# A recurrent attention followed by an MLP mixer: engine order taken from the order of the kernel's pieces

## The chip, the cores and the metric

The kernel runs on one core of a Trainium2 chip. Such a core has a matrix engine (PE, which also loads weights, shown as PEld), a vector engine (DVE), a scalar engine (ACT), a general engine (POOL) and a queue that only issues transfers here (SP). Each takes its own list of instructions; semaphores tie the lists together. The metric is the device time of one execution in microseconds (us).

## The reference

The first half is a linear attention with a decay for each channel (RWKV-6), for 4 batches, 8 heads, 768 tokens and 48 channels. The second half is an MLP mixer over tokens and then over channels. All in float32; the four weight matrices come as 64-bit floats.

```python
for t in range(S):
    cur = np.einsum('bhd,bhe->bhde', u[None] * kt, vt)
    y[:, :, t] = np.einsum('bhd,bhde->bhe', rt, state + cur)
    state = wt[:, :, :, None] * state + np.einsum('bhd,bhe->bhde', kt, vt)
...
xt = x.transpose(0, 2, 1)
h = np.maximum(xt @ w_tok1, 0.0) @ w_tok2
u = x + h.transpose(0, 2, 1)
h2 = np.maximum(u @ w_ch1, 0.0) @ w_ch2
return u + h2
```

## The kernel before, in words

**Attention units.** The 4 x 768 tokens are cut into 12 units of 256 tokens, three to a batch (NU is 12). A unit has two chunks c of 128 tokens, each of two halves of 64. Heads lie in pairs, so that most matmuls of the attention use quarter tiles of PE (64 x 64).

`levels(i)` builds, for unit i, the weights between tokens of one half: six levels, in each of which blocks of 1, 2, 4 ... 32 tokens are joined. `begin` makes on ACT the copies `rp` and `kp` (L195, L199) for level 0. `gram0` and `gram` (L211, L225) multiply k and r on PE into the PSUM tiles `gram` (pool ps_g, two buffers); `join` (L250 to L252) multiplies k and r in place by decays on DVE, so it has to come after the gram of its level and before the gram of the next; `pick` moves the products into `at`, on DVE for levels 0 to 3 (L217, L234) and on ACT for levels 4 and 5 (L242).

`post(i)` uses them. For each chunk, `tokens` transposes k on PE (L284) and copies it on ACT (L286, `kT`); `carry` multiplies it with v (L296, `kv_ps`) and then updates the state on DVE, a multiplication and an addition for each half (L303 to L306). Then `before` (L318) adds what earlier states give to `y_ps`, ACT copies one column (L324, `seen`), `within` (L331) adds the unit's own weights, and ACT writes the result to `x` (L334). `kv_ps` and `y_ps` share one PSUM buffer (ps_a, tag "a"). The last two pieces of post(i) issue the loads of unit i+3 on SP: six transfers of r, k and w and one of v, into the buffers that unit i used.

**Mixing.** For each batch: `hidden` (L353), `back` (L360, with an addition on DVE, L362), `turn` (a transpose, L367, copied by ACT, L368), `up` (L375, evicted by ACT, L377) and `down` (L384, added by DVE, L388, and stored from SP, L389). `up` and `down` go by three segments of 256 tokens.

**Weights.** `convert` brings one piece of a 64-bit matrix in by a transfer on SP into `d64` (two buffers) and makes it float32 with one operation of ACT (L155) and six of DVE (L156 to L161). There are 28 pieces: 3 of w_tok1, 4 of w_tok2, 9 of w_ch1 and 12 of w_ch2. All are converted during batch 0.

**Order.** Work is written as lists of pieces, each a cost and a function. `woven` merges lists so that each is spread evenly by its costs; `emit` calls the functions. Units 0 and 1 come first, then unit 2's levels woven with the posts of units 0 and 1, the hidden pieces of batch 0 and the conversion of w_tok1, then the rest of batch 0 woven with the other conversions. After that the mixing of each batch is woven with the attention of the next: three units with batch 0's last 52 us of matmuls, three with all of batch 1's and of batch 2's. Batch 3's mixing stands alone. In the kernel before, calling a piece only records its instructions. The framework's scheduler then chooses, for each engine, which of the instructions that are ready by its own planning goes next. So the order on an engine isn't that of the pieces: grams of one level lie cut in several runs between other matmuls, and joins of units 3 to 5 lie between the conversions.

```python
    p0, p1, p2 = post(0), post(1), post(2)
    p1[4:4] = hiddens[0] + hiddens[1]
    p2[4:4] = hiddens[2] + hiddens[3]
    emit(woven(levels(2), p0 + p1, to_tok1))
    emit(woven(p2[:-4], to_tok2[:2]))
    emit(p2[-4:-2] + hiddens[4] + p2[-2:] + hiddens[5])
```

Of the kernel before, what the change touches and what calls it, by code (L numbers as in the profile page):

```python
# [10 lines left out]
f32 = mybir.dt.float32  # L11
# [8 lines left out]
C = S // 128  # L20
UC = 2
# [13 lines left out]
def woven(*lists):  # L35

    keyed = []
    for n, pieces in enumerate(lists):
        total, at = sum(c for c, _ in pieces), 0.0
        for i, (c, f) in enumerate(pieces):  # L40
            keyed.append(((at + c / 2) / total, n, i, c, f))
            at += c
    return [(c, f) for *_, c, f in sorted(keyed, key=lambda e: e[:3])]


def emit(pieces):
    for _, f in pieces:
        f()


@with_exitstack
def rwkv6_then_mixer(
    ctx: ExitStack,
# [20 lines left out]

    nc = tc.nc
    pe, dve, act, pool, sp = nc.tensor, nc.vector, nc.scalar, nc.gpsimd, nc.sync

    const = ctx.enter_context(tc.tile_pool(name="const", bufs=1))
    wts = ctx.enter_context(tc.tile_pool(name="wts", bufs=1))
# [6 lines left out]
    ps_a = ctx.enter_context(tc.tile_pool(name="ps_a", bufs=1, space=bass.MemoryType.PSUM))  # L86
# [9 lines left out]
    def load_rkw(i):  # L96
        if i >= NU:
            return
        for n, t in enumerate((rs[i % 3], ks[i % 3], ws[i % 3])):
            for rows in (slice(0, 128),) if i < 3 else (slice(0, D), slice(P, P + D)):  # L100
                sp.dma_start(t[rows], rkw[i, n, rows, :])

    def load_v(i, queue=sp):
        if i >= NU:
            return
        vs[i] = vpool.tile([128, UC, DM], f32, name="vt")
        b, j = divmod(i, UB)
        queue.dma_start(vs[i], v[b, ts(j, UC * 128), :].rearrange("(c p) e -> p c e", p=128))

    u_col = const.tile([128, A], f32, name="u_col")  # L110
    act.dma_start(u_col, u)
    load_rkw(0)
    load_rkw(1)

# [56 lines left out]
    live = {}  # L171
# [98 lines left out]
    def post(i):  # L270
        bt, half = divmod(i, UB)
        at = weights_at[i % 3]
        r_, k_ = rs[i % 3], ks[i % 3]

        def tokens(c):
            if half == 0 and c == 0:
                xs[bt] = xpool.tile([128, C, DM], f32, name="x")
            L = live[i]
            if bt == 0:
                ps = ps_g.tile([128, 2, 512], f32, name="gram")[:, 0, :].rearrange("p (a t) -> p a t", a=A)  # L280
            else:
                ps = ps_m.tile([128, A, 128], f32, name="kT_ps", tag="m")
            for a in range(A):
                pe.transpose(ps[:, a, :], k_[:, ts(c * A + a, 128)], ident)  # L284
            L["kT"] = apool.tile([128, A, 128], f32, name="kT")
            act.copy(L["kT"], ps)  # L286

        def carry(c):
            L, vt = live[i], vs[i]
            ch = half * UC + c  # L290
            last = ch == C - 1
            kv = ps_a.tile([128, 2, 512], f32, name="kv_ps", tag="a")
            for a in range(A):
                for j, q in ((0, 0), (1, 1), (0, 1), (1, 0)):
                    if not (last and j == 1):
                        pe.matmul(kv[ts(q, P), j, ts(a, D)], L["kT"][ts(j, T), a, ts(q, P)],  # L296
                                  vt[ts(j, T), c, ts(2 * a + q, D)], start=True, stop=True)
            for j in range(1 if last else 2):
                g = 2 * ch + j
                new = apool.tile([128, A, D], f32, name="state", bufs=5)  # L300
                got = kv[:, j, :A * D].rearrange("p (a e) -> p a e", a=A)
                if g == 0:
                    dve.tensor_copy(new, got)  # L303
                else:
                    dve.tensor_mul(new, state[bt, g], L["w"][:, c, :, j].unsqueeze(2).to_broadcast([128, A, D]))
                    dve.tensor_add(new, new, got)  # L306
                state[bt, g + 1] = new

        pairs = ((0, 0), (1, 1), (1, 0), (0, 1))

        def before(c):

            ch = half * UC + c
            y = live[i]["y"] = ps_a.tile([128, 2, 512], f32, name="y_ps", tag="a")
            got = [(q, j) for q, j in pairs if 2 * ch + j > 0]
            for a in range(A):
                for q, j in got:
                    pe.matmul(y[ts(j, T), q, ts(a, D)], r_[q * P:q * P + D, ds((c * A + a) * 128 + j * T, T)],  # L318
                              state[bt, 2 * ch + j][q * P:q * P + D, a, :], start=(a == 0), stop=False,
                              skip_group_check=True)  # L320
            seen = apool.tile([128, 2], f32, name="seen")
            for j in range(2):
                if (0, j) in got:
                    act.copy(seen[ts(j, T)], y[ts(j, T), :, A * D - 1])  # L324

        def within(c):
            ch = half * UC + c
            vt, y = vs[i], live[i].pop("y")
            for a in reversed(range(A)):
                for q, j in pairs:  # L330
                    pe.matmul(y[ts(j, T), q, ts(a, D)], at[ts(j, T), q, c * A + a, :],  # L331
                              vt[ts(j, T), c, ts(2 * a + q, D)], start=(2 * ch + j == 0 and a == A - 1), stop=a == 0,
                              skip_group_check=True)
            act.copy(xs[bt][:, ch, :].rearrange("p (a q e) -> p q a e", a=A, q=2),  # L334
                     y[:, :, :A * D].rearrange("p q (a e) -> p q a e", a=A))

        pieces = []
        for c in range(UC):
            pieces += [(0.5, lambda c=c: tokens(c)), (0.5, lambda c=c: carry(c))]
        for c in range(UC):  # L340
            pieces += [(0.5, lambda c=c: before(c)), (1.0, lambda c=c: within(c))]
        return pieces + [(0.01, lambda: load_rkw(i + 3)), (0.01, lambda: load_v(i + 3))]
# [61 lines left out]
    hiddens, turned, ups, downs = mixing(0)  # L404
    hiddens = [list(e) for e in zip(*hiddens)]
    to_tok1, to_tok2 = conversion(wtok1, w_tok1, 2, 256), conversion(wtok2, w_tok2, 1, 384)
    to_ch1, to_ch2 = conversion(wch1, w_ch1, 1, 512), conversion(wch2, w_ch2, 1, 384)
    emit(woven(levels(0), levels(1)))
    load_v(0)
    load_rkw(2)  # L410
    load_v(1)
    load_v(2)
    p0, p1, p2 = post(0), post(1), post(2)
    p1[4:4] = hiddens[0] + hiddens[1]
    p2[4:4] = hiddens[2] + hiddens[3]
    emit(woven(levels(2), p0 + p1, to_tok1))
    emit(woven(p2[:-4], to_tok2[:2]))
    emit(p2[-4:-2] + hiddens[4] + p2[-2:] + hiddens[5])


    for bt in range(B):
        if bt == 0:
            emit(woven(turned, to_tok2[2:] + to_ch1[:3]))
            both = [f for e in zip(ups[0], ups[1]) for f in e]
            emit(woven(both, to_ch1[3:] + to_ch2[:6]))
            emit(woven(downs[0][:-4], to_ch2[6:]))
            pieces = downs[0][-4:] + ups[2] + downs[1] + downs[2]
        else:
            hiddens, pieces, ups, downs = mixing(bt)
            pieces = [(3.9, lambda h=h: emit(h)) for h in hiddens] + pieces + ups[0]  # L430
            for s in range(1, S // SEG):
                pieces += ups[s] + downs[s - 1]
            pieces += downs[-1]
        n = (bt + 1) * UB
        if n < NU:
            att = levels(n)
            for i in range(n, n + UB - 1):
                att += woven(levels(i + 1), post(i))
            att += post(n + UB - 1)
            emit(woven(att, pieces))  # L440
        else:
            emit(pieces)
# [29 lines left out]
```

## Time and profile before

| what | us |
|---|---|
| median of 3 runs (lowest, highest) | 694.05 (691.95, 696.34) |
| the profiled execution, its own time | 687.6 |
| its span in the trace | 685.6 |
| PE busy in the span | 641.6 (94%) |
| DVE busy | 293.1 (43%) |
| ACT busy | 194.8 (28%) |

The page's slices show how this is spread. Each digit is the busy share of one fortieth of the span (17 us) in tenths; PEclk is the clock that PE was granted.

```profile
PE   3889998996799999999999999999999999999998
DVE  5998899998821435442242305442132211000000
PEclk9997898998899999999999999999999999999999
```

PE is the fullest engine over the whole span, and DVE over the first eleven slices. The costliest groups are the matmuls of the channel mixing. A group's columns are line, engine, operation, output and inputs, shape and count, then busy time, the mean of one, and the idle time of the engine before it.

```profile
L375 PE MATMUL z_ps<-xT,wch 128*128 128x256 f32 x864 | 203.2, 389 | 3.5 <-DVE wch L161 3.0
L384 PE MATMUL h_ps<-wch,z 128*128 128x384 f32 x576 | 198.6, 498 | 3.7 <-DVE wch L161 3.5
L225 PE MATMUL gram<-r,k 48*64 48x32 f32 x3840 | 85.2, 235 | 13.1 <-DVE r L251 8.5
```

Matmuls overlap, so the mean duration of one is more than what it adds to the span; how many pass in a given time is read from the chain of waits or the order of time.

### The profile page before, as it was taken

To read this page: it belongs to the slowest core of one execution; us is meant where nothing else is said; L and a number is where in the kernel's file an instruction comes from. 1 tells how busy PE (TensorE), PEld (TensorE's weight loads), DVE (VectorE), ACT (ScalarE), POOL (GpSimd) and SP (SyncE) were. 2 spreads that over 40 slices of the span, in tenths; PEclk is the share of its full clock that TensorE was granted. 3 is DMA by queue.
4 is the path that set the end of the run, shared out by engine and by line. 5 is a ranking of instruction groups with operands and counts; after the bars stand their busy time and mean duration, and the time that the engine had idled before them with its cause. 6 is when DMAs were issued, how large, how long until landed. Compare 5 with 4: busy or idle time off the path is not lost.

```text
span 685.6 us, 18835 instructions
## 1 busy us (share of the span) xinstructions
PE 641.6 (94%) x8584; PEld 466.9 (68%) x8584; DVE 293.1 (43%) x585; ACT 194.8 (28%) x489; POOL 7.2 (1%) x32
## 2 busy tenths in 40 slices
PE   3889998996799999999999999999999999999998
PEld 3877656863586666788677656788677655786854
DVE  5998899998821435442242305442132211000000
ACT  7144533441242123432321303432211201220200
POOL 3000000000000000000000000000000000000000
PEclk9997898998899999999999999999999999999999
DMA  9244544332202131110210312000000000000000
GB/s 345 69 107 132 146 140 126 124 115 71 70 25 81 36 95 48 25 25 5 80 35 3 94 35 60 2 2 2 13 13 2 25 12 12 1 0 12 12 16 31
DMA packets 16111, 38.56 MB, mean 56 GB/s; under 512 B 2176, under 2 KB 8320, under 8 KB 16032
## 3 DMA queue, kind: packets, MB, share of 16 engines
q1 hardware_dynamic: 15888, 37.36, 17.9%
q8 instruction: 67, 1.10, 0.7%
q14 instruction: 12, 0.10, 0.0%
q10 hardware_dynamic: 144, 0.00, 0.0%
HBM read 32.64 MB, written 4.72 MB: 54 GB/s over the span
## 4 chain that ended last, share of the span: by engine, by line
PE 87%; DVE 9%; issue 2%; ACT 1%; DMA 1%; SPq 0%; DVEq 0%; ACTq 0%
PE z_ps L375 29%; PE h_ps L384 28%; PE gram L225 9%; PE h_ps L353 5%; PE h_ps L360 5%; PE y_ps L331 4%; PE kv_ps L296 2%; PE y_ps L318 2%; DVE r L251 1%; DVE k L250 1%; PE kT_ps L284 1%; PE gram L211 1%; PE xT_ps L367 1%; DVE at L217 1%; DMA w<-in_rkw_dram 1%
## 5 line engine op out<-in xcount | busy, mean ns | idle before, releaser
L375 PE MATMUL z_ps<-xT,wch 128*128 128x256 f32 x864 | 203.2, 389 | 3.5 <-DVE wch L161 3.0
L384 PE MATMUL h_ps<-wch,z 128*128 128x384 f32 x576 | 198.6, 498 | 3.7 <-DVE wch L161 3.5
L375 PEld LDWEIGHTS z_ps<-xT,wch 128*128 128x128 f32 x864 | 161.4, 192 | 28.4 <-DVE wch L161 3.2
L384 PEld LDWEIGHTS h_ps<-wch,z 128*128 128x128 f32 x576 | 107.9, 192 | 73.1 <-DVE wch L161 3.7
L377 ACT ACTIVATE z<-z_ps 128x256 f32<-128x256 f32 x144 | 55.1, 383 | 177.3 <-PE z_ps L375 177.2
L225 PEld LDWEIGHTS gram<-r,k 48*64 48x64 f32 x3840 | 76.5, 152 | 34.7 <-issue 24.3
L225 PE MATMUL gram<-r,k 48*64 48x32 f32 x3840 | 85.2, 235 | 13.1 <-DVE r L251 8.5
L388 DVE TENSOR_TENSOR o<-x,h_ps 128x384 f32<-128x384 f32 x24 | 13.3, 554 | 181.9 <-PE h_ps L384 181.9
L250 DVE TENSOR_TENSOR k<-k,decay 112x512 f32<-112x512 f32 x36 | 24.9, 691 | 62.2 <-PE gram L225 62.2
L242 ACT COPY at<-gram 16x256 f32<-16x256 f32 (+1 forms) x72 | 31.2, 434 | 44.7 <-PE gram L225 37.3
L250 DVE TENSOR_TENSOR k<-k,w 112x512 f32<-112x512 f32 x36 | 24.8, 688 | 39.6 <-PE gram L225 32.9
L360 PE MATMUL h_ps<-h,wtok 128*128 128x384 f32 x96 | 36.0, 503 | 1.8 <-DVE x L362 1.8
L353 PE MATMUL h_ps<-x,wtok 128*128 128x384 f32 x96 | 37.0, 520 | 0.0
L331 PEld LDWEIGHTS y_ps<-vt,at 64*64 64x64 f32 x768 | 26.2, 142 | 9.9 <-ACT seen L324 6.3
L234 DVE COPY_PREDICATED at<-mask,gram 128x512 f32<-128x512 uint8 x36 | 32.3, 897 | 0.0
L251 DVE TENSOR_TENSOR r<-r,w 112x512 f32<-112x512 f32 x36 | 24.7, 686 | 16.5 <-ACT rp L195 16.5
L331 PE MATMUL y_ps<-vt,at 64*64 64x48 f32 x768 | 29.2, 227 | 2.1 <-ACT seen L324 1.8
L211 PE MATMUL gram<-rp,kp 48*64 48x64 f32 x768 | 20.1, 246 | 11.1 <-ACT kp L199 8.0
L211 PEld LDWEIGHTS gram<-rp,kp 48*64 48x64 f32 x768 | 17.1, 154 | 16.4 <-ACT kp L199 10.4
L217 DVE COPY_PREDICATED at<-mask,gram 128x512 f32<-128x512 uint8 x24 | 16.7, 725 | 25.7 <-PE gram L211 25.4
L155 ACT ACTIVATE size<-d 128x384 f32<-128x384 f32 (+1 forms) x28 | 17.0, 608 | 28.2 <-DMA d<-in_w_ch_dram 13.3
L324 ACT COPY seen<-y_ps 64x2 f32<-64x2 f32 x44 | 6.8, 154 | 63.6 <-PE y_ps L318 63.3
(50 smaller groups left out, 429.1 us busy)
## 6 DMA issues: line engine op xcount, KB each, us to landing
vt<-in_v_dram SPq DMA_DIRECT2D x12, 384.0 KB, 3.9
d<-in_w_ch_dram SPq DMA_DIRECT2D x9, 512.0 KB, 3.6
d<-in_w_ch_dram SPq DMA_DIRECT2D x12, 384.0 KB, 3.0
out_dram<-o SPq DMA_DIRECT2D x24, 192.0 KB, 1.9
w<-in_rkw_dram SPq DMA_DIRECT2D x18, 192.0 KB, 3.5
k<-in_rkw_dram SPq DMA_DIRECT2D x18, 192.0 KB, 3.5
r<-in_rkw_dram SPq DMA_DIRECT2D x18, 192.0 KB, 3.4
r<-in_rkw_dram SPq DMA_DIRECT2D x3, 512.0 KB, 6.1
```

The costliest lines, as they stand in the source:

```text
L211: pe.matmul(g[cols, q, ts(a, T)], L["kp"][rows, tokens], L["rp"][rows, tokens], start=True, stop=True)
L225: fours(lambda q, j, rows, cols: pe.matmul(g[cols, q, ts(ca, 32)], k_[rows, ds(ca * 128 + j * T, T)], right[rows, ts(2 * ca + j, 32 // b), ...
L234: dve.copy_predicated(out=dst, data=g.rearrange("p q (m b) -> p q m b", b=b), mask=masks[l].rearrange("p x t -> p (x t)").rearrange("p (m ...
L242: act.copy(at[p:p + b, :, :, n * 2 * b + b:(n + 1) * 2 * b], g[p:p + b, :, :, ts(n, b)])
L250: dve.tensor_mul(left, left, wv[:, :, 1].unsqueeze(2).to_broadcast([ROWS, n, b]))
L251: dve.tensor_mul(right, right, wv[:, :, 0].unsqueeze(2).to_broadcast([ROWS, n, b]))
L331: pe.matmul(y[ts(j, T), q, ts(a, D)], at[ts(j, T), q, c * A + a, :], vt[ts(j, T), c, ts(2 * a + q, D)], start=(2 * ch + j == 0 and a == A ...
L353: pe.matmul(sums[i], wtok1[:, c, ts(i, 128)], xs[bt][:, c, :], start=(c == 0), stop=(c == C - 1))
L360: pe.matmul(ps, wtok2[:, i, ts(c, 128)], h1[:, i, :], start=(i == 0), stop=(i == DTOK // 128 - 1))
L375: pe.matmul(ps, wch1[:, m, ts(jt, 128)], xT[:, m, ts(s, SEG)], start=(m == 0), stop=(m == DM // 128 - 1))
L377: act.activation(zs[s][:, jt, :], ps, AF.Relu)
L384: pe.matmul(ps, zs[s][:, jt, ts(n, 128)], wch2[:, jt, :], start=(jt == 0), stop=(jt == NJ - 1))
```

## The change

`emit` moves into the kernel's function. After each piece, it looks at the instructions that the piece has recorded and ties each to the one before it on the same engine, with a dependency that needs no semaphore. So the scheduler can no longer choose: every engine's list, SP's and POOL's among them, is in the order of the pieces. What was recorded before the first piece (masks, first loads) is tied in the same way at the first call. The state update leaves `carry` and becomes a piece of its own, which `post` places one piece later. The insertion of the hidden pieces moves by two places for this. Last, one small ACT operation on a new tile `touched` stands ahead of the first loads, so that ACT's function table is loaded then.

```diff
-def emit(pieces):
-    for _, f in pieces:
-        f()
...
+    block = nc.cur_bb.bb
+    last, done = {}, len(block.instructions)
+    behind = mybir.DependencyInfo(mybir.DependencyClass.NoSync, mybir.DependencyReason.DATA)
+
+    def emit(pieces):
+
+        nonlocal done
+        for _, f in pieces:
+            f()
+            traced = block.instructions
+            for ins in traced[done:]:
+                if ins.engine in last:
+                    tc.add_manual_dep(ins, last[ins.engine], behind, reason="order of the pieces")
+                last[ins.engine] = ins.name
+            done = len(traced)
...
     act.dma_start(u_col, u)
+    touched = const.tile([1, 2], f32, name="touched")
+    dve.memset(touched, 0.0)
+    act.mul(touched[:, 1:], touched[:, :1], touched[:, :1])
     load_rkw(0)
     load_rkw(1)
...
-            kv = ps_a.tile([128, 2, 512], f32, name="kv_ps", tag="a")
+            kv = L["kv"] = ps_a.tile([128, 2, 512], f32, name="kv_ps", tag="a")
             for a in range(A):
                 for j, q in ((0, 0), (1, 1), (0, 1), (1, 0)):
                     if not (last and j == 1):
                         pe.matmul(kv[ts(q, P), j, ts(a, D)], L["kT"][ts(j, T), a, ts(q, P)],
                                   vt[ts(j, T), c, ts(2 * a + q, D)], start=True, stop=True)
-            for j in range(1 if last else 2):
+
+        def update(c):
+            L = live[i]
+            ch = half * UC + c
+            kv = L.pop("kv")
+            for j in range(1 if ch == C - 1 else 2):
                 g = 2 * ch + j
...
-        pieces = []
-        for c in range(UC):
-            pieces += [(0.5, lambda c=c: tokens(c)), (0.5, lambda c=c: carry(c))]
+        pieces = [(0.5, lambda: tokens(0)), (0.5, lambda: carry(0)), (0.5, lambda: tokens(1)), (0.1, lambda: update(0)),
+                  (0.5, lambda: carry(1)), (0.1, lambda: update(1))]
         for c in range(UC):
             pieces += [(0.5, lambda c=c: before(c)), (1.0, lambda c=c: within(c))]
...
-    p1[4:4] = hiddens[0] + hiddens[1]
-    p2[4:4] = hiddens[2] + hiddens[3]
+    p1[6:6] = hiddens[0] + hiddens[1]
+    p2[6:6] = hiddens[2] + hiddens[3]
```

## The prediction

> **What bounds the kernel now.** I read the span cut at its own milestones first, then the chain of waits, then the order of time on DVE and on SP. The stretches below end where the last weight is converted (183.9 us) and where the first matmul of each batch's token mixing stands in the chain (254.84, 411.90 and 568.80 us). Columns: the stretch, its length, busy time (instructions) of PE, weight load, DVE, ACT, POOL, then granted clock, DMA share, GB/s.
>
> ```profile
> 0.00:38.00 38.00, 24.42 (x772) 22.86 (x772) 28.97 (x57) 18.30 (x45) 6.32 (x24) 1.00 0.58 206
> 38.00:92.00 54.00, 48.42 (x1135) 37.11 (x1135) 47.39 (x103) 25.64 (x65) 0.33 (x3) 0.87 0.47 134
> 92.00:184.00 92.00, 76.37 (x967) 55.62 (x965) 84.76 (x169) 29.06 (x65) 0.00 (x0) 0.91 0.34 101
> 184.00:255.00 71.00, 69.65 (x931) 49.34 (x932) 22.94 (x49) 19.17 (x51) 0.33 (x3) 1.00 0.22 60
> 255.00:412.00 157.00, 155.99 (x2211) 111.97 (x2211) 53.06 (x102) 45.24 (x118) 0.22 (x2) 1.00 0.14 39
> 412.00:569.00 157.00, 155.42 (x2151) 111.49 (x2152) 49.29 (x96) 39.43 (x103) 0.00 (x0) 1.00 0.05 16
> ```
>
> From 255 us on, PE is busy 155 to 156 of 157 us: there is nothing for an order to fill. Before 184 us DVE is the fuller engine (84.76 of 92) and PE stands idle 35 us in all (38-24.4, 54-48.4, 92-76.4). So the change is decided in the first 184 us, by DVE. The order of time on DVE shows how a conversion costs two prices: alone, and mixed with other work.
>
> ```profile
> 111.51 0.69 DVE L161 SCALAR_TENSOR_TENSOR wch<-size,scale 128x512 f32<-128x512 f32 x1
> 112.12 0.42 DVE L156 TENSOR_SCALAR cut<-d 128x512 uint32<-128x512 uint32 x1
> ...
> 115.29 0.69 DVE L161 SCALAR_TENSOR_TENSOR wch<-size,scale 128x512 f32<-128x512 f32 x1
> ...
> 163.76 0.55 DVE L159 SCALAR_TENSOR_TENSOR scale<-d,scale 128x384 f32<-128x384 uint32 x1
> 165.66 0.69 DVE L250 TENSOR_TENSOR k<-k,decay 112x512 f32<-112x512 f32 x1 [1.36 <-PE gram L225]
> 166.27 0.55 DVE L160 TENSOR_TENSOR scale<-scale,cut 128x384 f32<-128x384 f32 x1
> ```
>
> Alone, a 512-wide conversion repeats every 3.78 us (111.51 to 115.29) and in the same way a 384-wide one every 3.11. The last three lines: L160 could have run at 164.2 and stood behind L250, which waited 1.36 us for PE.
>
> [...] Here independent operations follow each other every 0.60 us at 0.69 us of duration, dependent ones every 0.73; [...] SP's queue waited 49.0 us in 7 waits for y_ps L318, and what was behind waited too. [...]
>
> **The change part by part.** I compared the instruction order of both builds on each engine. It does change: on PE 347 runs of equal instructions become 294, and grams are no longer cut in pieces.
>
> *Table load.* Before, it runs from 1.23 to 2.51 us, and ACT then waits until 4.47 for r. In the new order it is still ACT's first operation. Cover: the r transfer; worth 0. Without that cover it would be worth at most 1.28.
>
> *Start.* The mask casts (1.59 and 0.58 us, now at 8.37 and 11.04, between the first joins and the first pick) move ahead of the w transfer that DVE awaits until 7.16 anyway. POOL now finishes mask by mask: about 0.8 + 1.63 + 3 x 0.87 = 5.0 us, so the casts fit. Gain **2** (0 to 3).
>
> *Units 0 to 2, 36 to 90 us.* I walk the new order with durations of the trace. ACT no longer runs unit 2's rp/kp (copies 0.65, four scalings 1.30 each) before unit 1's level 5 picks but after them, and the kT copies come behind: gram0 of unit 2 cannot start before about 42.8, its first pick before 43.4, while DVE has nothing else from 40.1: 3.3 us idle, and 1.2 just before. Then PE's order puts kv(1) before the y matmuls and those before gram(1). kv and y share one PSUM buffer (ps_a), kv(1) waits for the update of kv(0), which on DVE stands behind the two picks; this lasts to about 50.5, and DVE fills it with a whole conversion (3.8), so it costs DVE nothing. What costs it: the level 3 join waits for its gram, which stands behind unit 1's last kv (2), and unit 2's update waits after the last join for kT, its copy and kv (1.2). On PE, post(2)'s y waits until the last update at about 82.9, and its y, copies and four hidden matmuls take 7. Token mixing's second half (L360), at 85.4 before, comes at about **90**.
>
> *SP.* Each weight load now stands behind the loads of a unit, which wait until that unit's buffers are read. The second (behind load_rkw(3)) is issued at about 54 and lands at 58: DVE waits 2. The sixth stands behind load_rkw(5), which waits for unit 2's last y matmul at about 85.8; seven transfers of 0.39 us issue each go before it (2 MB in all, 5.6 us at the 347 GB/s of the first 20 us, and 3 us to land): **92.5**. Before, it was issued at 72.7 and converted by 84.5. DVE idles from 86 to 92.5 except for one addition. Bounds for these waits together: 10 to 30 us of DVE; I take 21.
>
> *Conversions.* At 92.5, 23 of 28 are left (before: 21 at 89.4): 9 x 3.78 + 14 x 3.11 = 77.6, and six additions of 0.5: the last ends at 92.5 + 80.6 = **173**, against 183.9, since joins and picks of units 3 to 5 no longer lie between. PE has 10 (L360, L367), 31 (z of two segments) and 12 us (18 matmuls of L384) to do in these 80 and is covered.
>
> *The tail of batch 0.* What DVE no longer did, PE has not done either. After 173 PE has left: 36 matmuls of z at 0.43 (two instructions, 0.2158 each in the chain's longest run, 31.08 us for 144) = 15.5; 54 of L384 at 0.645 = 34.8; three units at 10.5 (320 gram instructions at 0.0166 = 5.3, L211 1.1, kT 1.1, kv 1.0, y 2.0) = 31.4. Each change between full and quarter tiles costs: a stage of 157 us holds 142.7 of pure work in 89 runs, 0.16 each; the 60 runs here cost 9.6. Waits that PE has no cover for, as post(5) stands alone: kT copy before kv 0.7, update before the next kv 1.0, seen 0.5 twice, x copy 0.7, and two x copies in the middle of the stage, about 4.5. Sum **96**; hidden of batch 1 starts at 269 against 254.8: **+14**. The start's gain is in this.
>
> *Batches 1 and 2.* 80 runs instead of 89: 9 x 0.16 = 1.4 saved, and some 1.5 lost at the end of each stage, where filler no longer stands between kv, y and their copies. **0** (-3 to +3 for both). Batch 3 is unchanged: nothing is woven into it. Update pieces of their own add no instruction; POOL's memsets for w_chunk wait 351.5 us for DVE already and nobody waits for them.
>
> Sum: 685.6 + 14 = about 700 of span, 702 for that execution (687.6 before). The median of the runs shown is 694.05, 6.5 above the profiled one; from there, **708**.
>
> **Rivals.** *Faster: the waits vanish.* DVE's necessary work to the last conversion is 3 x 12.4 for levels, 7 for states, 95 for conversions, 3 for additions: 142. From 7.2 us on without a gap it ends at 150, the tail at 246: 9 less, and 4 from fewer runs: 681. For it: POOL, ACT and DMA are far from full. Against it: the sixth weight load alone stands behind unit 2's last y. It decides if DVE idles under 9 us before the last conversion. *No change*: 9 to 16 us of idle, as PE is full from 255 us on anyway: about 694 to 698. *Much slower*: in the tail 18 levels of a strict chain (join 1.3, gram 1.1, pick 0.6 to 1.1) also hold PE. I found filler matmuls of 1.3 to 3.2 us between grams, enough; if 0.8 us shows per level, 14 more: 722. *The order is not kept*: the built order excludes it.
>
> **How the numbers follow.** About 1%, 7 us, can be told from no change. My case (+7 to +22) 0.62, much slower 0.15, no change 0.17, faster 0.06. Range 694 to 722: it leaves out the faster case and the far end of the slow one. Slower 0.77, same 0.17, faster 0.06.
>
> **What would show it.** Right: DVE idle in 38 to 92 us grows to about 20; L155 or L156 waits for a weight DMA near 92; the last wch L161 near 173; first L353 of batch 1 near 269; later stages 157. Wrong: DVE full to 92 us, or L353 of batch 1 before 255, or a stage of batch 1 beyond 160.

## The result and the profile after

| | before | after |
|---|---|---|
| median (lowest, highest) of 4 runs each, side by side | 693.0 (689.3, 696.3) | 768.6 (767.5, 769.7) |
| ratio to before, 95% interval | 1 | 1.109 (1.103 to 1.116) |
| span of the profiled execution | 685.6 | 768.0 |

The kernel became 75.6 us slower. The forecast was 708, with 694 to 722 as its range: the direction was right and the size was five times too small. Both traces hold 18835 instructions, so the ties add none that could be seen.

First the slices of the page, to be read against those of the kernel before. Each digit is a fortieth of the span, now 19.2 us.

```profile
PE   3854886897799888998999998989999989999998
DVE  7855447999854342262414211443215210100000
PEclk9999786899799867999999998999999998999999
```

In the kernel before, PE's row is 9 from the twelfth slice on, but for the last. Now it has an 8 or a 7 in many slices and a 5 and a 4 in the third and fourth, and the clock row has dips up to the thirty-fourth slice. DVE's row has 4 and 4 in slices five and six, where the kernel before had 8 and 9.

Next the span of the kernel after, cut at the same milestones as in the prediction: the start of token mixing's second half (112), the last conversion (199), the first token mixing of batches 1, 2 and 3 (315, 484, 650). Columns as there: stretch, length, busy time (instructions) of PE, weight load, DVE, ACT and POOL, then clock, DMA share, GB/s.

```profile
0.00:38.00 38.00, 23.92 (x771) 22.74 (x772) 29.63 (x54) 13.36 (x33) 6.79 (x24) 1.00 0.45 172
38.00:112.00 74.00, 50.61 (x976) 39.10 (x976) 37.79 (x77) 18.79 (x48) 0.33 (x3) 0.88 0.31 81
112.00:199.00 87.00, 67.20 (x266) 45.23 (x269) 75.18 (x145) 27.81 (x64) 0.00 (x0) 0.84 0.41 126
199.00:315.00 116.00, 103.31 (x1858) 74.43 (x1854) 48.69 (x96) 26.91 (x72) 0.33 (x3) 0.85 0.16 40
315.00:484.00 169.00, 159.88 (x2164) 114.98 (x2161) 51.91 (x102) 44.33 (x116) 0.22 (x2) 0.96 0.14 37
484.00:650.00 166.00, 156.87 (x2135) 112.60 (x2134) 51.88 (x102) 43.69 (x115) 0.00 (x0) 0.97 0.06 17
650.00:768.00 118.00, 112.71 (x444) 79.57 (x440) 6.65 (x12) 18.13 (x45) 0.00 (x0) 1.00 0.03 11
```

Three things can be read here. In the second row no engine is full: 74 us hold 50.6 of PE and 37.8 of DVE. In the fourth PE stands idle 12.7 of 116 us at a clock of 0.85 (before, 1.3 of 71 us at 1.00). In the fifth and sixth PE is idle 9 us each and its busy time is up too, 159.9 and 156.9. The last row is as it was (118 us; 118.8 before): nothing is woven into it. The clock of the first two rows is to be read with care: up to about 83 us the column reads 1.00, though 64 gram instructions take 1.93 us there (at 77.13) and 1.14 at 83.08. The section on fillers at the start comes back to this.

The groups of PE, columns as before, show the same instruction counts at a higher price:

```profile
L392 PE MATMUL z_ps<-xT,wch 128*128 128x256 f32 x864 | 206.9, 392 | 9.3 <-ACT z L394 6.7
L401 PE MATMUL h_ps<-wch,z 128*128 128x384 f32 x576 | 207.3, 520 | 5.9 <-DVE wch L174 5.3
L238 PE MATMUL gram<-r,k 48*64 48x32 f32 x3840 | 80.4, 238 | 5.3 <-DVE at L247 2.0
```

L392 waits 6.7 us for its own eviction on ACT (before, all but 0.5 us of that group's idle time went to other waits). L401 is 8.7 us dearer (207.3 against 198.6) with no such wait; the run with fillers below, where it takes 194.2 and the end of batch 1's stage has a granted clock of 1.00, puts this down to the clock (0.79 for a dear run of L401, 471.0 to 481.5, here). The gram's waits fell from 13.1 to 5.3, an improvement.

### The profile page after: what moved, and what is told of

It reads as the page before. It is cut to its first block, busy times and chain, and to the rows that moved or that the text cites. A ratio compares the mean times of both kernels' runs of the same rounds, so it can differ in the third digit from the quotient of the medians.

```text
span 768.0 us, 18835 instructions
## 1 busy us (share of the span) xinstructions
PE 674.5 (88%) x8584; PEld 488.7 (64%) x8584; DVE 301.7 (39%) x586; ACT 193.0 (25%) x490; POOL 7.7 (1%) x32
## 4 chain that ended last, share of the span: by engine, by line
PE 77%; DVE 11%; ACT 5%; DMA 3%; issue 2%; POOL 1%; SPq 0%; DVEq 0%; ACTq 0%; POOLq 0%
PE h_ps L401 25%; PE z_ps L392 22%; PE gram L238 9%; PE h_ps L370 5%; PE h_ps L377 5%; PE y_ps L349 4%; PE kv_ps L309 2%; PE y_ps L336 2%; PE gram L224 2%; DMA d<-in_w_tok_dram 2%; DVE cut L170 1%; DVE scale L172 1%; DVE wch L174 1%; DMA d<-in_w_ch_dram 1%; PE kT_ps L297 1%
## 5 line engine op out<-in xcount | busy, mean ns | idle before, releaser
L392 PE MATMUL z_ps<-xT,wch 128*128 128x256 f32 x864 | 206.9, 392 | 9.3 <-ACT z L394 6.7
L401 PE MATMUL h_ps<-wch,z 128*128 128x384 f32 x576 | 207.3, 520 | 5.9 <-DVE wch L174 5.3
L392 PEld LDWEIGHTS z_ps<-xT,wch 128*128 128x128 f32 x864 | 162.5, 194 | 36.5 <-ACT z L394 11.0
L401 PEld LDWEIGHTS h_ps<-wch,z 128*128 128x128 f32 x576 | 115.1, 204 | 86.2 <-issue 12.5
L238 PE MATMUL gram<-r,k 48*64 48x32 f32 x3840 | 80.4, 238 | 5.3 <-DVE at L247 2.0
L377 PE MATMUL h_ps<-h,wtok 128*128 128x384 f32 x96 | 40.8, 555 | 6.8 <-ACT xT L385 5.3
L309 PE MATMUL kv_ps<-vt,kT 64*64 64x48 f32 x704 | 20.2, 254 | 24.2 <-DVE state L324 15.3
L309 PEld LDWEIGHTS kv_ps<-vt,kT 64*64 64x64 f32 x704 | 17.1, 166 | 30.9 <-issue 17.5
L349 PEld LDWEIGHTS y_ps<-vt,at 64*64 64x64 f32 x768 | 29.7, 159 | 10.2 <-ACT seen L342 7.6
L247 DVE COPY_PREDICATED at<-mask,gram 128x512 f32<-128x512 uint8 x36 | 32.2, 895 | 0.0
L377 PEld LDWEIGHTS h_ps<-h,wtok 128*128 128x128 f32 x96 | 18.0, 208 | 20.0 <-ACT xT L385 6.8
```

Of the source, the lines that this page charges most:

```text
L238: fours(lambda q, j, rows, cols: pe.matmul(g[cols, q, ts(ca, 32)], k_[rows, ds(ca * 128 + j * T, T)], right[rows, ts(2 * ca + j, 32 // b), ...
L247: dve.copy_predicated(out=dst, data=g.rearrange("p q (m b) -> p q m b", b=b), mask=masks[l].rearrange("p x t -> p (x t)").rearrange("p (m ...
L377: pe.matmul(ps, wtok2[:, i, ts(c, 128)], h1[:, i, :], start=(i == 0), stop=(i == DTOK // 128 - 1))
L392: pe.matmul(ps, wch1[:, m, ts(jt, 128)], xT[:, m, ts(s, SEG)], start=(m == 0), stop=(m == DM // 128 - 1))
L401: pe.matmul(ps, zs[s][:, jt, ts(n, 128)], wch2[:, jt, :], start=(jt == 0), stop=(jt == NJ - 1))
```

## The experiments

All times below are in us; every ratio is to the kernel before, run beside it on the same chip, with its 95% interval. The chips differ between groups of runs (the medians of the kernel before lie from 691.2 to 694.5), so a difference of two medians in the table is good to a few us. The milestones come from each run's trace, from the order of time on PE and DVE. A trace is of one execution: that of the kernel before took 687.6, under its median, and that of e2 was the fastest of its four (717.2). e1, as fast as the kernel before within 0.4%, has milestones 3 to 9 us later, so a difference of that size between two rows says little.

| run | what keeps the order of the pieces | median | ratio | second half of token mixing | last conversion | batch 1 begins | stages of batches 1, 2 |
|---|---|---|---|---|---|---|---|
| before | nothing | 693.0 | 1 | 85.3 | 183.9 | 254.8 | 157.1, 155.0 |
| after | all | 768.6 | 1.109 | 111.7 | 198.8 | 315.4 | 168.2, 166.9 |
| e1 | nothing | 695.7 | 1.004 (1.001 to 1.007) | 88.2 | 192.4 | 262.6 | 157.1, 155.0 |
| e2 | PE | 725.8 | 1.047 (1.038 to 1.056) | 92.7 | 173.4 | 274.1 | 161.0, 162.9 |
| e3 | DVE | 706.5 | 1.022 (1.015 to 1.030) | 99.2 | 182.4 | 277.2 | 157.1, 155.1 |
| e6 | ACT | 711.1 | 1.030 (1.024 to 1.036) | 94.7 | 174.4 | 270.1 | 160.3, 160.0 |
| e13 | SP | 714.2 | 1.031 (1.025 to 1.037) | 90.7 | 214.8 | 280.7 | 157.6, 155.2 |
| e4 | all but SP | 761.5 | 1.101 (1.092 to 1.109) | 107.9 | 190.8 | 308.7 | 168.3, 167.8 |
| e5 | all but ACT | 750.8 | 1.086 (1.079 to 1.093) | 108.1 | 197.3 | 307.4 | 162.2, 161.1 |
| e7 | all but DVE | 751.7 | 1.089 (1.082 to 1.095) | 100.4 | 187.1 | 301.7 | 166.6, 167.3 |
| e9 | all but PE | 738.5 | 1.071 (1.065 to 1.076) | 109.2 | 194.0 | 299.3 | 162.0, 158.3 |
| e14 | all but conversions | 744.7 | 1.074 (1.068 to 1.080) | 107.8 | 179.2 | 291.7 | 168.2, 166.9 |
| e15 | all but z evictions | 770.6 | 1.111 (1.106 to 1.117) | 115.9 | 198.3 | 317.3 | 168.1, 167.7 |
| e17 | all but rp and kp | 751.9 | 1.084 (1.077 to 1.092) | 110.0 | 194.2 | 304.7 | 163.9, 164.1 |
| e18 | all but state updates | 753.4 | 1.087 (1.079 to 1.096) | 105.0 | 189.4 | 302.7 | 165.9, 165.7 |

### One engine in order, or all but one

One edit, with a different set in each run. The update pieces, the moved insertion and the table load stay.

```diff
+    E = mybir.EngineType
+    ordered = {E.PE}
...
-                if ins.engine in last:
+                if ins.engine in ordered and ins.engine in last:
```

An empty set (e1), PE alone (e2), DVE alone (e3), ACT alone (e6), SP alone (e13):

> The changed kernel with the ordering taken out on every engine; update pieces and the early table load stay. If the ordering is what costs (both theories, that of PE's own order and that of DVE's and SP's order), this is the kernel before again: 693 us, within 5. If the separate update pieces cost by themselves, over 700.

> Only PE keeps the order of the pieces, the scheduler is free on DVE, ACT, POOL and SP. Theory A (PE's own order: matmuls of kv and y that wait stand in front of grams that could run, and each stall lets PE fall to half rate, a 64-instruction gram group taking 1.93 us for 1.06): most of the 75 us, 735 or more. Theory B (DVE's and SP's order: joins of units 3 to 5 wait for the last conversion, and loads stand behind loads): under 710.

> Only DVE keeps the order of the pieces. Theory B: 725 or more, with the joins of unit 3 starting after the last conversion and the first hidden matmul of batch 1 later than 275 us. Theory A: under 710.

> Only ACT keeps the order. If ACT's order costs by itself, 705 to 715. If it costs only where PE cannot pass over what waits for ACT, within 7 us of 694.

> Only SP's queue keeps the order of the pieces. If the engines' costs add up, SP is worth the 8 us that PE (31), ACT (17) and DVE (14) alone leave of the 75: about 703. If loads behind a unit's loads cost only together with the order of the engines that free those buffers, SP alone costs nothing: 692 to 697, and the last 8 us come from the interplay.

Without any order the rest of the change is worth 0.4%: the slowdown is the order. Each engine's order alone costs 2 to 5%, and 4.7 + 2.2 + 3.0 + 3.1 = 13.0% is more than the 10.9% of all together, so that part of it is shared. Neither theory of e2 and e3 held as a whole: PE alone cost less than theory A had (725.8, not 735 or more) and DVE alone less than theory B had (706.5, not 725 or more), though with DVE in order batch 1 did begin after 275 (277.2). ACT's 711.1 lay in its range. POOL's order was not tried alone.

SP was the surprise. Both numbers expected of it were wrong: it costs 22 us alone. The span of e13 by stretches shows where:

```profile
91.00:106.00 15.00, 9.52 (x148) 5.72 (x147) 11.25 (x23) 3.09 (x9) 0.00 (x0) 0.85 0.32 101
106.00:215.00 109.00, 90.76 (x1109) 64.00 (x1110) 93.47 (x186) 32.29 (x72) 0.00 (x0) 0.79 0.30 88
```

The weight loads of the first two matrices stand on SP behind the loads of units 3 to 5, which wait for their buffers; SP's list issues the remaining 21 of 28 only from 106.4 on, while the kernel before had 21 left to convert at 89.4. Joins of units 3 to 5 lie between them as in the kernel before: DVE is busy 93 of these 109 us, PE 91 at a clock of 0.79, and the last conversion ends at 214.8. Batch 1 begins 26 us late.

All but one: without SP's order (e4), ACT's (e5), DVE's (e7), PE's (e9).

> All engines but SP keep the order. If loads behind loads cost what the trace shows in front of the weight conversions (DVE waits of 9.6 us for these transfers and some of what follows from them), 755 or less, 10 to 20 us under the changed kernel. If the waits are taken over by others, within 5 us of 768.

> All engines but ACT keep the order. Theory C: with ACT in the order of the pieces, the eviction of a z tile and the kT copy stand behind the 3.9 us of a later unit's rp and kp, and PE waits for them; freeing ACT brings the stage of batch 1 from 168 us to 162 or less and the whole to 745 or less. Theory D (the coupling of PE's and DVE's orders, through one buffer of kv and y, is what is left): within 8 us of 768.

> All engines but DVE keep the order. Theory D: DVE is then free to put state updates ahead of conversions and to do joins of units 3 to 5 early, so PE's waits for kv go: 740 or less. Theory C: 755 or more.

> All engines but PE keep the order. PE alone in order cost about 31 us, DVE 12, ACT 17, and freeing SP, ACT or DVE gave back 7, 18 and 17. If the costs add up, this is about 735. If PE's order is what makes the others' orders costly, 715 or less.

None of them is the cause by itself: each gives back a part, PE the most (30 us), ACT and DVE 18 and 17 by the medians, SP 7. The 7 of SP are not clear of noise, as the intervals of e4 and of the kernel after (1.103 to 1.116) overlap. SP costs 22 alone and gives back little: with the other engines in order, the buffers that its loads wait for come free late anyway (r of unit 4 is issued at 65.8 before, at 85.2 in e4 and at 89.8 in the kernel after). Of the expectations, e9's sum of costs (about 735) came nearest; e5 brought the stage of batch 1 to 162 as theory C had it, but not the whole to 745; e4 and e7 fell between their two cases. The stages of batches 1 and 2 are as long as before with DVE or SP alone in order (157, 155), and 3 to 8 us longer with PE or ACT alone.

### The update back in carry

```diff
-        pieces = [(0.5, lambda: tokens(0)), (0.5, lambda: carry(0)), (0.5, lambda: tokens(1)), (0.1, lambda: update(0)),
-                  (0.5, lambda: carry(1)), (0.1, lambda: update(1))]
+        pieces = [(0.5, lambda: tokens(0)), (0.5, lambda: (carry(0), update(0))), (0.5, lambda: tokens(1)),
+                  (0.5, lambda: (carry(1), update(1)))]
```

The insertions go back to `[4:4]` with it; the order is kept on all engines.

> The changed kernel, every engine ordered, with the state update back in the piece of its carry (hidden pieces inserted two places earlier, as before). If the separate update piece costs PE its waits (an update stands behind picks or a conversion on DVE, and the next kv waits in the one buffer of ps_a), 760 or less. If the separate piece helps (the second half's transposes are issued before the wait), 770 or more.

764.9, ratio 1.108 (1.100 to 1.115), between its two cases and not to be told from the kernel after (1.103 to 1.116). Its trace shows where time moved: the second half of token mixing starts at 105.8 and the last conversion ends at 188.3, 6 and 10 us earlier than in the kernel after, but batch 1 begins at 314.8 as there. Whether the placing of the update one piece later helps or harms is left open.

### Which instructions: four freed groups

An instruction whose name is in a set `free` is tied to nothing; all others keep the order of the pieces. Each run fills the set from one function. For conversions (e14):

```diff
+                if ins.name in free:
+                    continue
                 if ins.engine in last:
...
+        begun = len(block.instructions)
         n = dst.free_size()
...
+        free.update(ins.name for ins in block.instructions[begun:])
```

e15 frees ACT's evictions of z, e17 ACT's copies and scalings `rp` and `kp`, e18 the state updates on DVE.

> As the kernel after, but whatever a conversion records (its load on SP, its operation on ACT, its six on DVE) is tied to nothing; all the rest keeps the order of the pieces. If the first stretch is long because conversions wait for their loads ahead of state updates and picks, token mixing's second half starts before 98 us (111.7 in the kernel after), and the whole is 745 to 755. If it is long by PE's own order (gram, kv, y, each behind the other), it starts at 105 to 112 and the whole stays over 760.

> As the kernel after, but ACT's evictions of z in channel mixing are tied to nothing. If the stages of batches 1 and 2 are long because these stand behind the scalings for level 0, a stage takes 161 to 163 us instead of 167 to 168 and the whole 756 to 760. If they are long by waits for kT, state and seen, a stage stays at 166 to 168 and the whole over 764.

> As the kernel after, but ACT's copies and scalings for level 0 (rp and kp) are tied to nothing. If ACT's order costs by these standing ahead of z evictions and behind picks, a stage of batches 1 and 2 takes 161 to 164 us instead of 167 to 168, the first gram of unit 2 waits less (7.9 us in the kernel after), and the whole is 748 to 758. If it costs by kT, seen and x copies standing behind evictions, stages stay at 166 to 168 and the whole over 762.

> As the kernel after, but the state updates on DVE are tied to nothing. If the 10 us wait of kv_ps for the state in unit 1 is what lengthens the first stretch, token mixing's second half starts at 98 to 104 us (111.7 in the kernel after) and the whole is 755 to 762. If something else is late next (the weight that DVE waits for, the picks), it starts later than 107 and the whole stays over 764.

**Conversions (e14)** give back 24 us by the medians, but not in the way expected: the second half of token mixing still starts at 107.8, as the rival had it. The gain is on DVE. Its stretches in e14:

```profile
38.00:108.00 70.00, 51.74 (x977) 39.57 (x978) 50.64 (x107) 21.44 (x52) 0.42 (x3) 0.85 0.47 126
108.00:179.00 71.00, 61.74 (x356) 43.41 (x355) 60.95 (x119) 24.80 (x58) 0.00 (x0) 0.97 0.35 108
```

DVE now does 50.6 us of work before 108 (37.8 in the kernel after): its holes are filled by conversions, and the last one ends at 179.2, not 198.8. The stages of batches 1 and 2 don't change at all.

**State updates (e18)** give back 15. The order of time on DVE of the kernel after (start, duration, what; in brackets the idle time before it and what ended it) shows the stall that they make in the first stretch:

```profile
64.12 0.69 DVE L247 COPY_PREDICATED at<-mask,gram 128x512 f32<-128x512 uint8 x1
69.01 0.43 DVE L169 TENSOR_SCALAR cut<-d 128x512 uint32<-128x512 uint32 x1 [4.19 <-DMA d<-in_w_tok_dram]
...
72.18 0.69 DVE L174 SCALAR_TENSOR_TENSOR wtok<-size,scale 128x512 f32<-128x512 f32 x1
72.78 0.35 DVE L323 TENSOR_TENSOR state<-state,w_chunk 128x192 f32<-128x192 f32 x1
```

and on PE of the same kernel, where the last thing done ahead of this line ended at 64.6:

```profile
74.52 1.10 PE L309 MATMUL kv_ps<-vt,kT 64*64 64x48 f32 x32 [9.95 <-DVE state L324]
```

The update stands behind a whole conversion, and that conversion behind its load. DVE waits 4.2 us for the transfer and works 3.8 on the conversion while PE waits 10 us for an update of four operations of 0.35 (72.78 to 74.37). And the load is late because of SP's order (issues on SP, kernel after):

```profile
9.54 0.37 SPq L162 DMA_DIRECT2D d<-in_w_tok_dram  x1
57.45 0.81 SPq L111 DMA_DIRECT2D r<-in_rkw_dram  x2
...
60.66 0.98 SPq L162 DMA_DIRECT2D d<-in_w_tok_dram  x2
```

From 9.9 to 57.45 SP issues nothing: load 2 of the weights stands behind those of unit 3, which wait for unit 0's last y. It lands at 69.0. Three lists meet in this one stall: SP's, DVE's and PE's. In e4, with SP free, the same conversion starts at 64.41 without a wait, and PE waits 5.7 us, not 10. With the updates free the wait of kv_ps for the state falls from 11.8 to 1.4 between 38 us and the second half of token mixing, which starts 6.7 earlier: less than 10, as other waits stay (5.9 us of kv_ps for kT, 3.1 of y_ps for `seen`) and that of y_ps for the state grows from 1.3 to 2.2.

**Scalings (e17)** give back 17, **evictions (e15)** nothing: 1.111 (1.106 to 1.117) against 1.109 of the kernel after. Both runs were meant for one stall of batches 1 and 2. ACT in the kernel after:

```profile
344.59 0.38 ACT L394 ACTIVATE z<-z_ps 128x256 f32<-128x256 f32 x1 [0.30 <-PE z_ps L392]
344.87 0.65 ACT L208 COPY rp<-r 112x512 f32<-112x512 f32 x1
345.42 0.68 ACT L208 COPY kp<-k 112x512 f32<-112x512 f32 x1
345.98 1.32 ACT L212 ACTIVATE rp<-r,u_col 112x128 f32<-112x128 f32 x4
347.20 1.30 ACT L212 ACTIVATE kp<-k,u_col 112x128 f32<-112x128 f32 x4
348.41 0.36 ACT L394 ACTIVATE z<-z_ps 128x256 f32<-128x256 f32 x1
```

and PE at that time:

```profile
342.99 2.86 PE L392 MATMUL z_ps<-xT,wch 128*128 128x256 f32 x12
345.69 0.60 PE L297 MATMUL kT_ps<-ident,k 128*128 128x128 f32 x4
348.82 4.54 PE L392 MATMUL z_ps<-xT,wch 128*128 128x256 f32 x12 [2.53 <-ACT z L394]
```

The second z of the pair done at 345.7 is evicted at 348.41, behind 3.5 us of copies and scalings, and the next pair waits for its PSUM buffer. The price is double: 2.53 us of waiting and then 4.54 us for work that took 2.86 just before, at a granted clock of 0.63 (348.8 to 353.4). In e17 the scalings lie in the holes of ACT, the same matmuls follow the same transposes without a wait,

```profile
336.30 0.60 PE L302 MATMUL kT_ps<-ident,k 128*128 128x128 f32 x4
336.94 2.86 PE L397 MATMUL z_ps<-xT,wch 128*128 128x256 f32 x12
```

and a stage takes 164. That is the smaller part of what e17 saves. Of 17.8 us of span, 7.1 lie in these two stages; the last conversion ends 4.5 us earlier, and from there to batch 1 it takes 110.4 for 116.6. The 7.9 us wait of a gram that e17's text gives to unit 2 is that of unit 0, which starts at 7.94 us; unit 2's first gram did not wait on PE for `kp`. In e15 the wait of 2.4 us is still there: with the evictions tied to nothing the scheduler still put this one behind the scalings.

### Filling PE to keep its clock

The dearer L401 suggested PE's clock. This run adds matmuls of two identity matrices where PE has waits for a copy or an update in the tail of batch 0 and at the ends of stages; they compute nothing that is used.

```diff
+    def busy(n):
+        ps = ps_m.tile([128, 128], f32, name="busy_ps", tag="m")
+        for _ in range(n):
+            pe.matmul(ps, ident, ident, start=True, stop=True)
...
+        if i == 4 or i > UB and i % UB == UB - 1:
+            for at_, n in ((5, 5), (4, 5), (1, 4)):
+                pieces.insert(at_, (0.01, lambda n=n: busy(n)))
...
+            if i == 4 or i > UB and i % UB == UB - 1:
+                pieces[-1:-1] = [(0.01, lambda: busy(3))]
+                pieces += [(0.01, lambda: busy(3))] if c == 0 else []
```

> The changed kernel (every engine ordered) with 79 matmuls added on PE that compute nothing (a unit matrix on itself, into a spare buffer of ps_m), 3 to 5 at a time, in front of kv and y matmuls of units 4, 5, 8 and 11, where PE stood waiting. If stalls cost only their own length, this is the same as 768 or up to 10 us slower. If stalls cost above all through the clock that PE loses (24 instructions of L401 take 9.4 to 10.4 us after a row of stalls and 7.94 otherwise), these runs come back to 8 us and the whole is 6 to 15 us faster, though PE does more.

The kernel has 92 added matmuls (184 instructions), not the 79 of that text. It took 757.9, ratio 1.096 (1.089 to 1.104). The two groups of e8 that matter:

```profile
L412 PE MATMUL h_ps<-wch,z 128*128 128x384 f32 x576 | 194.2, 494 | 4.2 <-DVE wch L174 3.9
L286 PE MATMUL busy_ps<-ident 128*128 128x128 f32 x184 | 26.2, 284 | 0.0
```

PE does 26 us more by the sum of durations, and L412 (the L401 of the kernel after) falls from 207.3 to 194.2. The second of the two expectations came true. Where the dearer ones came from can be seen at the end of batch 1's stage in the kernel after:

```profile
467.11 0.67 PE L309 MATMUL kv_ps<-vt,kT 64*64 64x48 f32 x16 [1.74 <-DVE state L324]
468.22 0.77 PE L336 MATMUL y_ps<-state,r 48*64 48x48 f32 x32 [0.45 <-DVE state L324]
469.47 1.94 PE L349 MATMUL y_ps<-vt,at 64*64 64x48 f32 x32 [0.48 <-ACT seen L342]
471.34 10.05 PE L401 MATMUL h_ps<-wch,z 128*128 128x384 f32 x24
```

Three short waits, 2.7 us within 5, and the next 24 full-size matmuls take 10.05 us; such runs of 24 take 7.91 to 8.01 elsewhere in the stage. The runs at 279.5, 299.8 and 455.5 take 10.42, 10.48 and 9.46 in the same way; with the fillers e8's runs at 275.9, 294.3, 446.9 and 462.1 take 7.91 to 8.01. The granted clock (before the last two columns) agrees; the stretch of these 24 in the kernel after, then the end of the same stage in e8:

```profile
471.00:481.50 10.50, 10.50 (x44) 5.93 (x44) 0.07 (x1) 0.48 (x1) 0.00 (x0) 0.79 0.01 2
446.00:486.00 40.00, 39.03 (x458) 26.32 (x452) 9.44 (x18) 6.67 (x19) 0.00 (x0) 1.00 0.36 79
```

In the 10 us before each of these four runs in the kernel after no single wait of PE was longer than 1.74 us: two to four waits of 0.45 to 1.74 us stood there. And in e11 below, 30 us in which PE was busy without a gap did not raise the rate (a gram still takes 1.93).

Two freedoms and the fillers together (e16: conversions, z evictions, `busy`):

> Both freedoms of the two runs before, and the 92 added matmuls of the run with a busy PE. If the three are separate costs (first stretch 15 to 20, evictions 10, clock 10), the whole is 728 to 740. If they are one cost seen three times, it is not under 745.

734.3, ratio 1.060 (1.054 to 1.065), in the range of three separate costs, though one of the three, the evictions, had turned out to be worth nothing. Against e14, run beside it (1.074, 1.068 to 1.080), the fillers again bring 10.4 us, as they brought 10.7 to the kernel after: late conversions and the clock are separate costs. In e16's span by stretches the tail runs at 0.98 of the clock (0.87 in e14) and takes 105 us.

### The same fillers at the start

Grams of units 0 and 1 also seemed to run at half rate (1.93 us per 64 against 1.06 to 1.16 later). e11 puts 3 full matmuls behind each of the grams of levels 1 to 5 and more where PE waits, in the kernel after; e12 puts the former alone into the kernel before.

```diff
+            if i < 2:
+                busy(3)
...
+        for at_, n in {0: ((5, 6), (3, 8), (1, 18)), 1: ((3, 30), (1, 4))}.get(i, ()):
+            pieces.insert(at_, (0.001, lambda n=n: busy(n)))
+            if i == 0:
+                pieces[-1:-1] = [(0.001, lambda: busy(3))]
+                pieces += [(0.001, lambda: busy(3))]
...
-    p1[6:6] = hiddens[0] + hiddens[1]
+    p1[8:8] = hiddens[0] + hiddens[1]
```

> The changed kernel with 108 matmuls that compute nothing on PE between 10 and 75 us: 3 after each gram of levels 1 to 5 of units 0 and 1, and 3 to 30 in front of the kv and y matmuls of units 0 and 1. If the waits alone set this stretch, no change (768) or slower. If the half rate of PE sets it too (a gram group takes 1.93 us for 1.06 there), L377 starts before 107 us (now 111.7) and the whole is 3 to 10 us faster.

> The kernel before (no ordering) with 30 such matmuls, 3 after each gram of levels 1 to 5 of units 0 and 1. Before, PE ran at half rate there (a gram group 1.97 us), and DVE waited 2.5 us for grams. If the rate is kept, 2 to 4 us faster than before; if these matmuls delay grams, the same or slower.

Both got slower: 781.0, ratio 1.133 (1.127 to 1.139), and 701.3, 1.016 (1.011 to 1.021). The fillers did not do what they were for, as PE's order of time in e11 shows:

```profile
46.37 1.93 PE L243 MATMUL gram<-r,k 48*64 48x32 f32 x64
48.23 1.65 PE L191 MATMUL busy_ps<-ident 128*128 128x128 f32 x6
49.67 1.06 PE L304 MATMUL gram<-ident,k 128*128 128x128 f32 x4
50.52 5.08 PE L191 MATMUL busy_ps<-ident 128*128 128x128 f32 x36
55.54 0.68 PE L316 MATMUL kv_ps<-vt,kT 64*64 64x48 f32 x32
...
58.52 1.16 PE L229 MATMUL gram<-rp,kp 48*64 48x64 f32 x64
```

PE is busy all of 20 to 50 us and a gram still takes 1.93; only after 5 us of full-size matmuls in a row kv takes 0.68 (1.10 in the kernel after, at 43.11) and a gram of level 0 1.16 (1.99 there, at 45.19). That such durations go with a low clock, e12 shows: its trace has the clock there, and for the same durations (1.93 and 1.65 us) it was half.

```profile
20.00:37.00 17.00, 17.00 (x360) 15.54 (x354) 10.83 (x19) 1.33 (x2) 0.00 (x0) 0.50 0.02 4
```

In e11 the column reads 1.00 for 20 to 50 us, in the kernel after up to about 86 and in the kernel before up to 48.5, whatever the durations. By the durations, the kernel after ran at the low rate up to 83 us (a gram 1.93 at 77.13, 1.14 at 83.08), the kernel before only up to about 42 (kv 1.11 at 39.46, 0.66 at 42.80); both fell to it again later, for the first time at 86.5 to 101 and at 49 to 55, where the column reads 0.50. From the first kT to the first token mixing, e11 needs 38.3 us (49.7 to 88.0), the kernel after 38.1 (37.5 to 75.6). But e11's fillers take PE's time there too, so what the clock costs in this stretch isn't shown.

## Why the prediction was wrong

**Right.** The table load and the new pieces are worth about nothing (e1, +0.4%). The conversions are contiguous and take 82.0 us from the sixth load (116.8) to the last (198.8); 80.6 was forecast. What DVE puts off, PE must do in a tail: with PE, ACT or DVE alone in order it took 100.7, 95.7 and 94.8 us, against a forecast of 96 and 70.9 before. Batch 3 is unchanged. The first suspicion, that the sixth weight load stands behind unit 2's last y, held: DVE waits for that load at 116.84:

```profile
116.84 0.36 DVE L169 TENSOR_SCALAR cut<-d 128x384 uint32<-128x384 uint32 x1 [2.98 <-DMA d<-in_w_tok_dram]
```

The start's gain of 2 does not show: the first transposes of k stand at 37.1 before and at 37.5 after. And a sign of being wrong that the prediction named came: a stage of batch 1 beyond 160 (168.2).

Three steps make up the miss: the last conversion came 25.8 us later than forecast, the tail took 20.6 longer, and the two stages 23.0. Together these are 69 us; the span, 768, exceeds the forecast 700 by 68.

**The step that failed first: "Units 0 to 2, 36 to 90 us".** It put token mixing's second half at 90; it came at 111.7, and so "SP: 92.5" became 116.8 and 173 became 198.8. Of the 24.3 us by which "SP" missed, 21.6 are the late end of unit 2's last y from states (107.4, forecast 85.8); the load took 9.4 from there, not 6.7. The walk costed the waits of unit 0 and did well there: kv(1) waited until 49.0, forecast 50.5. For unit 1 it took the second weight's lateness as "DVE waits 2" and a conversion between kv and update as costing DVE nothing. But the conversion was itself waiting for a load, with the update behind it, and PE behind the update: 10 us of PE at 64.6, of which e18 gives back 6.7 in this stretch. Freeing DVE gives back 11.3 there, ACT, PE and SP some 3 each, conversions 4, where differences of 3 or 4 between single traces say little: the 21.7 us are several waits in a row. How they divide in full, and how much of them is the low rate of PE up to 83 us, wasn't settled.

**Second: "The tail of batch 0. Sum 96".** It was 116.6. Waits of PE without cover were put at 4.5; PE stood idle 12.7. That is 8 of the 21 us. Another part is a term that the sum didn't have: the clock, 0.85 in that stretch. With fillers it is 0.98 (e16; 0.87 in e14 without them), and the tail is 6 to 7 us shorter (110.2 in e8 for 116.6, 105.3 in e16 for 112.6 in e14), though the fillers take time themselves. The remainder was not measured apart.

**Third: "Batches 1 and 2: 0 (-3 to +3 for both)".** They became 11 and 12 us longer each (168.2 and 166.9 for 157.1 and 155.0). The step counted runs on PE and did not walk ACT's list there: z evictions stand behind 3.5 us of scalings. e17 takes 3 to 4 us off a stage by that alone, e8 1 to 4 with the clock at 1.00 and 0.99 (0.96 and 0.97 in the kernel after); which waits make up the remainder stays open. The argument that PE, full from 255 us on, left an order nothing to fill was true, but said only that it could not gain. It does not follow that it could not lose.

**The rivals.** "Much slower, 722" had the right sign and the wrong mechanism: the grams' own chain wasn't what grew. In the tail grams waited 1.5 us for joins, where that rival had 14. "Faster" needed DVE to idle under 9 us before the last conversion; in 38 to 112 alone it idled 36.

**Shown and not shown.** That the order by itself makes the slowdown, and that it comes through all four lists, is shown. Late conversions (e14, 24 us), scalings (e17, 17), updates (e18, 15) and the clock (e8, 11) are shown one by one as differences of medians; that they add up was tried only for conversions and clock. No version with an order on any engine beat the kernel before.

## What to carry to other kernels

An order by hand is to be walked on every engine and every queue at once: ask of each short operation that another engine waits for what long operation, and what load, stands just ahead of it. A full engine in the profile means that a change of order can't gain there, not that it can't lose. And count a stall of the matrix engine twice: it can cost its own length and then a slow stretch of matmuls after it (here 2.53 us of waiting, then 4.54 us for what took 2.86).

## What was not expected of the hardware

- Short waits were followed by matmuls at a lower rate: after three of 0.45 to 1.74 us within some 5 us, 10.05 us for 24 instructions of L401 against 7.91 to 8.01; after one of 2.53 us, 4.54 against 2.86 for 12 of L392.
- In e11, thirty microseconds without a gap of quarter-tile grams (1.93 us per 64) and groups of three full-tile matmuls did not raise the rate; after 5.1 us of full-tile matmuls in a row it was up (1.16 for 64 of level 0, 1.99 in the kernel after). Why the one counts and the other doesn't stays open.
- The clock column can mislead early in a trace: e11's shows 1.00 in that slow stretch, e12's 0.50 for grams and fillers of the same durations. There the durations are to be trusted.
